# An attention output's last third visits four column strips of TensorE in turn, with new scheduler keys

## The chip, the cores and the metric

One core of a Trainium2 chip. The metric is the device time of one execution in microseconds (us), lower is better.

## The reference

A gated linear attention over 4 batches, 8 heads, 768 positions and head size 48, followed by two feed-forward layers (384 to 2048 to 384) over the 3072 tokens:

```python
for t in range(S):
    state = alpha[:, :, t, :, None] * state + np.einsum('bhd,bhe->bhde', k[:, :, t], v[:, :, t])
    y[:, :, t] = np.einsum('bhd,bhde->bhe', q[:, :, t], state)
...
h = x @ w_in
sp = np.where(h > 20.0, h, np.log1p(np.exp(np.minimum(h, 20.0))))
g = h * np.tanh(sp)
return (g @ w_out).astype(np.float32)
...
h = np.maximum(x @ w_in, 0.0)
return (h * h @ w_out).astype(np.float32)
```

## The kernel before, in words

**Attention.** The 768 positions are cut into 6 chunks `c` of 128; each chunk is done for each of the 4 batches `b`, 24 units (c, b) in all. For one unit, `a_load` and `a_loadv` fetch alpha, k, q (tile `akq`) and v; `a_prep`, `a_inv` and `a_k` run scans and products over them on VectorE (DVE; tiles `P`, `akq`); `a_kT` transposes k on TensorE; `a_scores` multiplies k by q and DVE masks the result into two tiles `at`, one for the even heads and one for the odd; `a_y` (line 538) makes the chunk's output on TensorE; `a_u` updates the state `st`; `a_x` splits the output into two halves `xh` and `xl`, which the first feed-forward layer reads.

**`a_y`.** The output of a unit is 384 rows, made as three thirds (`kk` = 0, 1, 2) of 128 rows by 128 positions in one PSUM bank. Each third is four strips of 32 rows (`i` = 0 to 3), and a strip is computed with 32 of TensorE's 128 columns. A strip of the first two thirds holds 32 rows of one head: for c > 0 one matmul with the state (`akq,st` in the profile) and one with the scores (`at,v`). A strip of the last third holds the remaining 16 rows of two heads: one matmul with the state and two with the scores. In chunk 0 there is no state, and only the matmuls with scores are made. All operands are 32-bit floats, and the trace has two records for each such matmul, here called two passes. So a unit of c > 0 has 28 matmuls and 56 passes, 32 of them in the first two thirds and 24 in the last; there are 20 such units.

**Feed-forward.** Weights come as 64-bit floats; `w_load`, `w_sign`, `w_abs`, `w_bits` and `w_split` turn a pair of weight blocks into `whi` and `wlo` (ScalarE, ACT, and DVE; tile `raw` before that). A step (c, f) is one block of 128 hidden units for one chunk: `h_mm` makes nine matmuls into one of three banks `ph`; `mish1`, `mish2` (ACT) and `mish3` (DVE: `u`, `y`, then `g`, which reads the bank last) apply the activation; `split_hi` and `split_lo` make `gh` and `gl`; `out1` adds nine matmuls to banks `pc`. The second layer follows after all 96 steps of the first, with `relu1` and `out2`.

**What sets the order.** Nothing is issued directly. `Recorder` notes each call as a unit of work with a cost from `price` (line 347), its queue (P TensorE, V VectorE, A ScalarE, G GpSimd, S the DMA queue) and a key. `Plan.order` (line 245) then plays the queues forward by these costs: of the units that could start within `SLACK` of the earliest, the one with the smallest key goes next. The keys are step numbers plus the offsets in the tables `FIRST_AT`, `EARLY_AT`, `LATER_AT`, `WEIGHT_AT` and `MLP_AT` (lines 36 to 41). All instructions are issued from line 321, so the profile's rows carry L321 and are told apart by their tiles.

The order of the passes of `a_y` is that of the loops `for kk`, `for i`, state first, then `for h in heads`.

Of the kernel before, what the change touches and what calls it, by code (L numbers as in the profile page):

```python
# [17 lines left out]
B, H, S, D = 4, 8, 768, 48  # L18
DM, DFF = 384, 2048
NT = B * S  # L20
CH = 128
# [5 lines left out]
CUT = ((slice(0, 32), slice(0, 32), slice(32, 64)), (slice(16, 48), slice(32, 64), slice(0, 32)))  # L27
# [2 lines left out]
WAIT = 0.2  # L30
SWITCH = 0.3
BYTE_SHIFTS = range(8)
SLACK = dict(P=4.68, V=0.01, A=0.18, G=0.10, S=3.45)


FIRST, EACH = -14.34, 4.47
FIRST_AT = dict(a_load=-8.92, a_loadv=-0.87, a_prep=-25.04, a_inv=-1.22, a_k=-40.25, a_kT=16.99, a_scores=-42.12, a_flag=-25.48, a_y=-7.03, a_u=-55.34, a_x=19.72)
EARLY_AT = dict(a_load=86.48, a_loadv=0.29, a_prep=-2.05, a_inv=1.20, a_k=-0.59, a_kT=-39.22, a_scores=-50.37, a_flag=29.17, a_y=-26.49, a_u=-16.63, a_x=-15.63)
LATER_AT = dict(a_load=-106.20, a_loadv=-63.70, a_prep=-101.21, a_inv=20.99, a_k=37.87, a_kT=-78.32, a_scores=-75.84, a_flag=23.67, a_y=2.78, a_u=-20.53, a_x=-24.76, b_load=-9.08, p_load=53.41)
WEIGHT_AT = dict(w_load=-16.99, w_sign=-7.37, w_abs=-52.56, w_bits=-0.61, w_split=-4.57)  # L40
MLP_AT = dict(mish1=42.39, mish2=0.64, mish3=1.90, hi=1.97, lo=-28.42, out=0.86)
EXP20 = 485165195.40979
NG = NF // 2

# [157 lines left out]
class Plan:  # L202
# [42 lines left out]
    def order(self):  # L245
        units = self.units
        users = {name: {i for i, _, _ in self.uses[name]} for name in self.tag_of}
        left = {name: len(x) for name, x in users.items()}
        nth, made, begun, freed = {}, {}, {}, {}
        for u in units:  # L250
            for name in u["new"]:
                tag = self.tag_of[name][0]
                nth[name] = made.get(tag, 0)
                made[tag] = nth[name] + 1
        held = [[] for _ in units]
        for name, x in users.items():
            for i in x:
                held[i].append(name)
        after = [[] for _ in units]
        for i, u in enumerate(units):  # L260
            u["after"] -= u["deps"]
            for j in u["deps"] | u["after"]:
                after[j].append(i)
        wait = [len(u["deps"] | u["after"]) for u in units]
        start, done, base = ([0.0] * len(units) for _ in range(3))
        free = dict.fromkeys("PVAGS", 0.0)
        shared, mode = 0.0, None
        ready = {q: {i for i, u in enumerate(units) if u["queue"] == q and not wait[i]} for q in free}

        def buffers(i):  # L270

            t, seen = 0.0, {}
            for name in units[i]["new"]:
                tag, bufs = self.tag_of[name]
                n = begun.get(tag, 0) + seen.get(tag, 0)
                seen[tag] = seen.get(tag, 0) + 1
                if nth[name] != n or len(freed.get(tag, [])) <= n - bufs:
                    return None
                if n >= bufs:
                    t = max(t, sorted(freed[tag])[n - bufs])  # L280
            return t

        for _ in units:
            picks = []
            for q, pool in ready.items():
                found = []
                for i in pool:
                    t = buffers(i)
                    if t is not None:
                        found.append((max(free[q], base[i], t, shared if units[i]["port"] else 0.0), units[i]["key"], i))  # L290
                if found:
                    first = min(found)[0]
                    pick = min((x for x in found if x[0] <= first + SLACK[q]), key=lambda x: x[1:])
                    picks.append((first, q, pick))
            _, q, (t, _, i) = min(picks, key=lambda x: x[0])
            u = units[i]
            ready[q].discard(i)
            start[i] = t
            free[q] = t + u["cost"] + (SWITCH if u["mode"] != mode and q == "P" else 0.0)
            mode = u["mode"] or mode  # L300
            done[i] = free[q] + u["late"]
            if u["port"]:
                shared = free[q] + (0.08 if q == "V" else 0.0)
            for name in u["new"]:
                tag = self.tag_of[name][0]
                begun[tag] = begun.get(tag, 0) + 1
            for name in held[i]:
                left[name] -= 1
                if not left[name]:
                    freed.setdefault(self.tag_of[name][0], []).append(max(done[j] for j in users[name]))  # L310
            for j in after[i]:
                base[j] = max(base[j], done[i] if i in units[j]["deps"] else start[i])
                wait[j] -= 1
                if not wait[j]:
                    ready[units[j]["queue"]].add(j)
        return sorted(range(len(units)), key=lambda i: start[i])
# [30 lines left out]
def price(queue, op, args, kw):  # L347


    out = args[0]  # L350
    n = out.free_size()
    ins = [a for a in (*args[1:], *kw.values()) if hasattr(a, "ap") and a is not kw.get("accum_out")]
    wide = [a for a in ins if a.space != PSUM and a.free_size() > 8]
    if queue == "P":
        if op == "transpose":
            return 0.109, 0.2, False
        m, n = args[1].free_size(), args[2].free_size()
        if args[2].dtype == F32R:
            return n / 2200, 0.2, False
        return (0.085 if m == 32 else 0.052 if n == D else 0.107), 0.28, False  # L360
    if queue == "S":
        size = math.prod(out.shape) * mybir.dt.size(out.dtype)
        return size / 390e3, 2.7, False
    if queue == "A":
        return (0.06 if len(wide) < len(ins) else 0.11) + n / 1200 + (0.1 if "accum_out" in kw else 0), 0.13, False
    if queue == "V":
        if op == "memset":
            return 0.03, 0.07, False
        if op == "reciprocal":
            return 0.07 + n * 0.006, 0.11, False  # L370
        if "scan" in op:
            return n * 2.21e-3, 0.11, True
        if op == "tensor_scalar" and out.space != PSUM and len(wide) == len(ins):
            return 0.07 + n / 1920, 0.11, True
        return 0.072 + n / 960, 0.11, len(wide) > 1
    if op == "tensor_scalar":
        return 0.12 + n / 1024, 0.05, True
    if op == "memset":
        return 0.1 + n / 1200, 0.05, False
    return 0.1 + n * 2.3e-3, 0.05, True  # L380
# [14 lines left out]
def fast_kernel(ctx, tc, flags, akq, v, w1i, w1o, w2i, w2o, out):  # L395
    nc = Plan(tc.nc)
# [21 lines left out]
    st = const.tile([128, B, NP, 2, D], F32, name="st")  # L418
# [49 lines left out]
    vt, At, Pt, kT, at, yt, kt, qt, v0 = {}, {}, {}, {}, {}, {}, {}, {}, []  # L468
# [69 lines left out]
    def a_y(c, b):  # L538
        ps = abank(c, 2)
        for kk in range(NK):  # L540
            for i in range(4):
                o = ps[32 * i:32 * i + 32, CH * kk:CH * kk + CH]
                heads = (4 * kk + i,) if kk < 2 else (2 * i, 2 * i + 1)
                if c > 0:
                    p = heads[0] // 2
                    s2 = st[:, b, p, heads[0] % 2, CUT[heads[0] % 2][0]] if kk < 2 else st[:, b, p].rearrange("p j e -> p (j e)")[:, 32:64]
                    nc.tensor.matmul(o, s2, qt[c, b][:, p, :], start=True, stop=False, skip_group_check=True)
                for h in heads:
                    p, j = h // 2, h % 2
                    w = vt[c, b][:, h, CUT[j][1] if kk < 2 else CUT[j][2]]  # L550
                    nc.tensor.matmul(o, w, at[c, b, j][:, p, :], start=(c == 0 and h == heads[0]), stop=(h == heads[-1]), skip_group_check=True)
        yt[c, b] = ps

    def a_u(c, b):
# [151 lines left out]
    with tc.manual_schedule():  # L706
# [13 lines left out]
        def at_step(t, fn, *args, key=None):  # L720
            name = fn.__name__
            if key is None:
                c, b = args[0], args[1] if len(args) > 1 else 0
                if c == 0 and name[0] == "a":
                    key = FIRST + EACH * b + FIRST_AT[name]
                else:
                    key = t + (EARLY_AT if 0 < c < 3 and name[0] == "a" else LATER_AT)[name]
            slots.setdefault(math.floor(t), []).append((fn, args, key))
# [64 lines left out]
        for s in range(tot + LAG):  # L793
            ph = s // NA
            if s < tot:
                c, f = step(s)
                run(h_mm, 2 * ph, c, f, key=s)
                run(relu1 if ph else mish1, c, f, key=s + MLP_AT["mish1"])
            p = s - 1
# [6 lines left out]
            o = s - LAG  # L806
# [61 lines left out]
```

## Time and profile before

| | |
|---|---|
| time, median of 3 runs | 965.78 us (963.88 to 966.77) |
| the profiled execution: time, span | 966.28 us, 964.6 us |
| mean granted TensorE clock | 0.982 of full speed |
| busy: TensorE, its weight loads, DVE, ACT | 97%, 82%, 66%, 58% of the span |
| chain that ended last | TensorE 83%, ACT 7%, DVE 7% |

The span runs from the first to the last instruction. TensorE's busy time is a union of overlapping matmuls, so a busy TensorE can still be slow. Where the engine waited, a row says so in brackets, with what ended the wait.

### The profile page before, as it was taken

The numbers are of one execution on the slowest core, as the hardware profiler recorded it, in microseconds if no ns is written. First come the engines' busy times: TensorE is split into PE (matmuls) and PEld (weight loads), VectorE is DVE, ScalarE is ACT, GpSimd is POOL, SyncE is SP. The second block draws the span as 40 slices with busy tenths as digits, with TensorE's granted clock in tenths as the row PEclk, the third lists the DMA queues.
The fourth block names the chain that finished last, engine by engine and source line by source line (L and its number), as shares of the span: only waits on it lengthen the run. The fifth ranks groups of instructions, "written<-read, shape, count | busy, mean of one in ns | idle before, by whom it ended". The sixth has DMA issues, their size and how long they took to land.

```text
span 964.6 us, 14441 instructions
## 1 busy us (share of the span) xinstructions
PE 934.1 (97%) x5818; PEld 788.5 (82%) x5818; DVE 637.3 (66%) x1014; ACT 559.6 (58%) x1103; POOL 2.7 (0%) x10
## 2 busy tenths in 40 slices
PE   6888999999999999999999999999999999999996
PEld 5666777778888888878888889988999899999995
DVE  7899999998788887777679997343333343433332
ACT  4487998778666767677599865332332332422322
POOL 1000000000000000000000000000000000000000
PEclk7699999999999999999999999999999999999998
DMA  8145324340221211121032251010000100100001
GB/s 326 68 154 191 126 66 137 121 149 1 82 82 47 77 45 45 44 78 45 1 138 92 70 194 64 1 66 1 33 33 1 66 1 1 66 1 1 34 1 36
DMA packets 22075, 67.13 MB, mean 70 GB/s; under 512 B 1776, under 2 KB 4848, under 8 KB 22000
## 3 DMA queue, kind: packets, MB, share of 16 engines
q1 hardware_dynamic: 22000, 66.13, 19.6%
q8 instruction: 47, 0.77, 0.3%
q14 instruction: 28, 0.23, 0.1%
HBM read 55.90 MB, written 10.22 MB: 69 GB/s over the span
## 4 chain that ended last, share of the span: by engine, by line
PE 83%; ACT 7%; DVE 7%; issue 1%; DMA 1%; SPq 0%; DVEq 0%; ACTq 0%
PE ph L321 37%; PE pc L321 34%; PE pa L321 12%; ACT u L321 2%; ACT y L321 2%; ACT raw L321 1%; DVE akq L321 1%; ACT whi L321 1%; DVE raw L321 1%; DMA raw<-w1o 1%; DVE P L321 1%; DVE st L321 1%; ACT gh L321 1%; DVE gl L321 1%; ACT akq L321 1%
## 5 line engine op out<-in xcount | busy, mean ns | idle before, releaser
L321 PE MATMUL ph<-xh,wlo 128*128 128x512 f32 x576 | 230.1, 399 | 5.3 <-DVE g L321 2.7
L321 PE MATMUL ph<-xh,whi 128*128 128x512 f32 x576 | 228.0, 396 | 0.0
L321 PE MATMUL ph<-xl,whi 128*128 128x512 f32 x576 | 227.9, 396 | 0.0
L321 DVE TENSOR_TENSOR gl<-g,gh 128x512 fp32r<-128x512 f32 x192 | 131.9, 687 | 127.2 <-ACT gh L321 126.7
L321 ACT ACTIVATE u<-ph 128x512 f32<-128x512 f32 x192 | 113.8, 593 | 170.0 <-PE ph L321 163.4
L321 ACT ACTIVATE gh<-g 128x512 fp32r<-128x512 f32 x192 | 120.2, 627 | 135.1 <-PE pa L321 112.8
L321 DVE TENSOR_TENSOR g<-u,ph 128x512 f32<-128x512 f32 x96 | 66.0, 687 | 118.6 <-ACT u L321 118.6
L321 PEld LDWEIGHTS ph<-xh,wlo 128*128 128x128 f32 x576 | 108.7, 189 | 28.7 <-DVE g L321 4.4
L321 PEld LDWEIGHTS ph<-xh,whi 128*128 128x128 f32 x576 | 108.5, 188 | 25.4
L321 PEld LDWEIGHTS ph<-xl,whi 128*128 128x128 f32 x576 | 108.5, 188 | 20.6
L321 PE MATMUL pc<-gh,wlo 128*128 128x512 f32 x288 | 117.0, 406 | 0.9 <-ACT x L321 0.9
L321 PE MATMUL pc<-gh,whi 128*128 128x512 f32 x288 | 113.6, 394 | 0.0
L321 PE MATMUL pc<-gl,whi 128*128 128x512 f32 x288 | 113.1, 393 | 0.0
L321 DVE SCALAR_TENSOR_TENSOR u<-u,y 128x512 f32<-128x512 f32 x96 | 65.8, 686 | 50.4 <-ACT y L321 50.1
L321 PE MATMUL pc<-wlo,gh 128*128 128x384 f32 x288 | 97.0, 337 | 0.0
L321 PE MATMUL pc<-whi,gh 128*128 128x384 f32 x288 | 97.0, 337 | 0.0
L321 PE MATMUL pc<-whi,gl 128*128 128x384 f32 x288 | 96.9, 337 | 0.0
L321 DVE SCALAR_TENSOR_TENSOR g<-y,ph 128x512 f32<-128x512 f32 x96 | 65.4, 681 | 1.6
L321 PEld LDWEIGHTS pc<-gh,wlo 128*128 128x128 f32 x288 | 54.1, 188 | 14.8 <-ACT x L321 1.3
L321 DVE SCALAR_TENSOR_TENSOR y<-u,y 128x512 f32<-128x512 f32 x96 | 65.7, 685 | 0.7
L321 PEld LDWEIGHTS pc<-gh,whi 128*128 128x128 f32 x288 | 54.0, 187 | 13.2
L321 PEld LDWEIGHTS pc<-gl,whi 128*128 128x128 f32 x288 | 54.1, 188 | 12.1 <-DVE gl L321 0.6
(90 smaller groups left out, 1261.6 us busy)
## 6 DMA issues: line engine op xcount, KB each, us to landing
akq<-akq SPq DMA_DIRECT2D x20, 770.5 KB, 4.5
raw<-w1i SPq DMA_DIRECT2D x8, 768.0 KB, 4.6
v<-v SPq DMA_DIRECT2D x24, 256.0 KB, 4.4
raw<-w1o SPq DMA_DIRECT2D x8, 768.0 KB, 4.3
raw<-w2i SPq DMA_DIRECT2D x8, 768.0 KB, 4.4
raw<-w2o SPq DMA_DIRECT2D x8, 768.0 KB, 4.3
x2d<-x SPq DMA_DIRECT2D x7, 768.0 KB, 3.5
x<-x2d SPq DMA_DIRECT2D x7, 768.0 KB, 4.3
```

What stands on the lines that cost most here:

```text
L321: method(*args, **kw)
```

## The change

`a_y` is written with the strips in the inner loop: for each third, the four state matmuls, then the first scores matmul of each strip, then (last third only) the second scores matmul of each strip. The number, shape and operands of the matmuls are the same. The price of a 32-column matmul in `price` falls from 0.085 to 0.06; a TensorE unit that depends on another TensorE unit may now follow it at once (before, 0.2 or 0.28 us later); and `SLACK`, `FIRST`, `EACH` and the five tables of keys have new numbers.

```diff
-SLACK = dict(P=4.68, V=0.01, A=0.18, G=0.10, S=3.45)
+SLACK = dict(P=7.05, V=0.00, A=0.15, G=0.10, S=5.68)
...
-FIRST, EACH = -14.34, 4.47
+FIRST, EACH = -14.93, 4.00
...
-                base[j] = max(base[j], done[i] if i in units[j]["deps"] else start[i])
+                same = units[j]["queue"] == "P" == u["queue"]
+                base[j] = max(base[j], free["P"] if same else done[i] if i in units[j]["deps"] else start[i])
...
-        return (0.085 if m == 32 else 0.052 if n == D else 0.107), 0.28, False
+        return (0.06 if m == 32 else 0.052 if n == D else 0.107), 0.28, False
...
-            for i in range(4):
-                o = ps[32 * i:32 * i + 32, CH * kk:CH * kk + CH]
-                heads = (4 * kk + i,) if kk < 2 else (2 * i, 2 * i + 1)
-                if c > 0:
-                    p = heads[0] // 2
-                    s2 = st[:, b, p, heads[0] % 2, CUT[heads[0] % 2][0]] if kk < 2 else st[:, b, p].rearrange("p j e -> p (j e)")[:, 32:64]
-                    nc.tensor.matmul(o, s2, qt[c, b][:, p, :], start=True, stop=False, skip_group_check=True)
-                for h in heads:
+            groups = [(4 * kk + i,) if kk < 2 else (2 * i, 2 * i + 1) for i in range(4)]
+            o = [ps[32 * i:32 * i + 32, CH * kk:CH * kk + CH] for i in range(4)]
+            for i, heads in enumerate(groups if c > 0 else ()):
+                p, j = heads[0] // 2, heads[0] % 2
+                s2 = st[:, b, p, j, CUT[j][0]] if kk < 2 else st[:, b, p].rearrange("p j e -> p (j e)")[:, 32:64]
+                nc.tensor.matmul(o[i], s2, qt[c, b][:, p, :], start=True, stop=False, skip_group_check=True)
+            for n in range(len(groups[0])):
+                for i, heads in enumerate(groups):
+                    h = heads[n]
                     p, j = h // 2, h % 2
                     w = vt[c, b][:, h, CUT[j][1] if kk < 2 else CUT[j][2]]
-                    nc.tensor.matmul(o, w, at[c, b, j][:, p, :], start=(c == 0 and h == heads[0]), stop=(h == heads[-1]), skip_group_check=True)
+                    nc.tensor.matmul(o[i], w, at[c, b, j][:, p, :], start=(c == 0 and n == 0), stop=(h == heads[-1]), skip_group_check=True)
```

What this does to the order of the instructions is shown at three places. In these rows `xN` is N equal instructions in a row, and the numbers tell the tiles apart.

**TensorE, the first unit of chunk 1: the last third of `a_y`.** `pa` is the output's bank, `st` the state, `at_197` the scores of the even heads and `at_198` those of the odd. Before (the last strip of the second third, then the last third):

```order
L321 MATMUL pa_209<-akq_159,st_109 32x128
L321 MATMUL pa_209<-at_198,v_160 32x128
L321 MATMUL pa_209<-akq_159,st_109 32x128
L321 MATMUL pa_209<-at_197,v_160 32x128
L321 MATMUL pa_209<-at_198,v_160 32x128
L321 MATMUL pa_209<-akq_159,st_109 32x128
L321 MATMUL pa_209<-at_197,v_160 32x128
L321 MATMUL pa_209<-at_198,v_160 32x128
```

Now (from the second third's scores on):

```order
L322 MATMUL pa_209<-akq_159,st_109 32x128 x4
L322 MATMUL pa_209<-at_197,v_160 32x128
L322 MATMUL pa_209<-at_198,v_160 32x128
L322 MATMUL pa_209<-at_197,v_160 32x128
L322 MATMUL pa_209<-at_198,v_160 32x128
L322 MATMUL pa_209<-akq_159,st_109 32x128 x4
L322 MATMUL pa_209<-at_197,v_160 32x128 x4
L322 MATMUL pa_209<-at_198,v_160 32x128 x4
```

Before, a strip of the last third has its three matmuls (six passes) in a row, and the next strip follows; now each strip has one matmul (two passes) at a time. In the first two thirds it was two matmuls (four passes) in a row, and is now one.

**DVE, around 130 us: the `g` of step 14 (`g_343`), after which the bank `ph_335` is free for step 17.** Before:

```order
L321 TENSOR_TENSOR gl_340<-g_337,gh_339 128x512
L321 TENSOR_TENSOR wlo_347<-raw_315,whi_346 128x768
L321 SCALAR_TENSOR_TENSOR u_336<-u_336,y_338 128x512
L321 SCALAR_TENSOR_TENSOR P_390<-akq_373,reset_108 128x516
L321 SCALAR_TENSOR_TENSOR y_338<-u_336,y_338 128x512
L321 RECIPROCAL reset_108<-P_390 128x4
L321 SCALAR_TENSOR_TENSOR u_342<-u_342,y_344 128x512
L321 SCALAR_TENSOR_TENSOR g_343<-y_338,ph_335 128x512
```

Now:

```order
L322 SCALAR_TENSOR_TENSOR u_336<-u_336,y_338 128x512
L322 SCALAR_TENSOR_TENSOR raw_333<-raw_333 128x768
L322 TENSOR_TENSOR gl_340<-g_337,gh_339 128x512
L322 SCALAR_TENSOR_TENSOR y_338<-u_336,y_338 128x512
L322 SCALAR_TENSOR_TENSOR u_342<-u_342,y_344 128x512
L322 SCALAR_TENSOR_TENSOR g_343<-y_338,ph_335 128x512
```

The scan that makes `P` (named SCALAR_TENSOR_TENSOR here, TENSOR_TENSOR_SCAN in the trace) and its reciprocal no longer stand ahead of this `g`. Counted to this `g`, DVE's queue holds 197 instructions before and 193 now: those missing are one scan `P`, one reciprocal, one scan back over `akq` and one small memset. Counted to the `g` that frees a bank for step 8, it holds the same 138 in both.

**The DMA queue (SP), its first loads.** Before:

```order
L321 DMA raw<-w1i 128x2x768
L321 DMA v<-v 128x512
L321 DMA raw<-w1i 128x2x768
L321 DMA akq_136<-akq 128x517
L321 DMA akq_136<-akq 128x512 x2
```

Now:

```order
L322 DMA raw<-w1i 128x2x768
L322 DMA akq_136<-akq 128x517
L322 DMA akq_136<-akq 128x512 x2
L322 DMA v<-v 128x512
L322 DMA raw<-w1i 128x2x768
```

The first `v`, which the first `a_y` of all reads, now stands behind the three loads of the third batch's alpha, k and q.

## Rows read from the trace of the kernel before

**Rows 1.** The page, part 1: busy time, share of span, instructions.

```profile
PE 934.1 (97%) x5818; PEld 788.5 (82%) x5818; DVE 637.3 (66%) x1014; ACT 559.6 (58%) x1103; POOL 2.7 (0%) x10
```

**Rows 2.** Stretches: length, busy of PE, PEld, DVE, ACT, POOL, granted clock, DMA.

```profile
45.00:100.00 55.00, 48.90 (x471) 38.04 (x471) 51.98 (x87) 43.96 (x89) 0.00 (x0) 0.99 0.47 163
100.00:150.00 50.00, 47.93 (x275) 37.68 (x275) 48.63 (x73) 47.94 (x96) 0.00 (x0) 1.00 0.33 110
150.00:205.00 55.00, 53.20 (x439) 41.78 (x438) 52.99 (x91) 43.56 (x90) 0.00 (x0) 1.00 0.34 119
205.00:480.00 275.00, 275.00 (x1983) 221.67 (x1982) 215.96 (x362) 191.19 (x391) 0.00 (x0) 1.00 0.16 54
```

**Rows 3.** Waits of PE from 45 to 205 us: total, times, longest.

```profile
PE ph L321 <- DVE g L321: 2.7, 3, 1.2
PE ph L321 <- DVE wlo L321: 2.5, 4, 1.1
PE pa L321 <- DVE at L321: 2.2, 2, 1.4
```

**Rows 4.** Timeline of PE, one a_y at 304.71: start, length, operation.

```profile
304.71 0.45 PE L321 MATMUL pa<-akq,st 128*32 128x128 f32 x8
304.95 0.42 PE L321 MATMUL pa<-at,v 128*32 128x128 f32 x8
305.17 0.44 PE L321 MATMUL pa<-akq,st 128*32 128x128 f32 x8
305.39 0.44 PE L321 MATMUL pa<-at,v 128*32 128x128 f32 x8
305.60 0.38 PE L321 MATMUL pa<-akq,st 128*32 128x128 f32 x2
...
305.83 0.30 PE L321 MATMUL pa<-akq,st 128*32 128x128 f32 x1
...
306.08 0.30 PE L321 MATMUL pa<-akq,st 128*32 128x128 f32 x1
...
306.33 0.30 PE L321 MATMUL pa<-akq,st 128*32 128x128 f32 x1
...
306.54 0.63 PE L321 MATMUL pa<-at,v 128*32 128x128 f32 x6
307.10 0.38 PE L321 MATMUL pa<-v,kT 128*64 128x48 f32 x6
```

**Rows 5.** The unit's first weight loads in the timeline, and all 480 by line.

```profile
304.70 0.18 PEld L321 LDWEIGHTS pa<-akq,st 128*32 128x32 f32 x8 [0.37 <-issue]
...
L321 PEld LDWEIGHTS pa<-akq,st 128*32 128x32 f32 x480 | 22.2, 108 | 9.7 <-issue 5.8 <-DVE at L321 3.9
```

**Rows 6.** Two stretches, PE's matmuls on the state alone: busy (passes).

```profile
45.00:100.00 55.00, 8.10 (x96) 0.99 0.47 163
205.00:480.00 275.00, 24.18 (x288) 1.00 0.16 54
```

**Rows 7.** Stretch of the third a_y of chunk 0, columns as in rows 2.

```profile
26.00:28.50 2.50, 2.42 (x32) 1.56 (x32) 2.50 (x6) 0.48 (x2) 0.00 (x0) 0.51 0.10 36
```

**Rows 8.** Timeline of DVE and PE near 133 us.

```profile
130.59 1.22 DVE L321 TENSOR_TENSOR_SCAN P<-akq,reset 128x516 f32<-128x516 f32 x1
...
132.98 0.68 DVE L321 SCALAR_TENSOR_TENSOR g<-y,ph 128x512 f32<-128x512 f32 x1
...
133.71 0.50 PE L321 MATMUL ph<-xh,wlo 128*128 128x512 f32 x1 [1.21 <-DVE g L321]
```

**Rows 9.** Timeline of DVE and PE near 93 us (step 8).

```profile
92.30 0.68 DVE L321 SCALAR_TENSOR_TENSOR g<-y,ph 128x512 f32<-128x512 f32 x1
...
93.03 0.50 PE L321 MATMUL ph<-xh,wlo 128*128 128x512 f32 x1 [1.20 <-DVE g L321]
```

**Rows 10.** An early stretch (columns as in rows 2) and the first a_y.

```profile
9.00:15.00 6.00, 4.74 (x66) 3.53 (x62) 5.36 (x9) 4.27 (x10) 0.00 (x0) 0.72 1.03 401
...
11.28 1.86 PE L321 MATMUL pc<-at,v 128*32 128x128 f32 x32
```

More of the change, by code (lines that the diff above doesn't have):

```diff
@@ L32 @@
 BYTE_SHIFTS = range(8)
-SLACK = dict(P=4.68, V=0.01, A=0.18, G=0.10, S=3.45)
-FIRST, EACH = -14.34, 4.47
[L37 to L41, printed above, removed]
+SLACK = dict(P=7.05, V=0.00, A=0.15, G=0.10, S=5.68)
+FIRST, EACH = -14.93, 4.00
+FIRST_AT = dict(a_load=-8.68, a_loadv=0.02, a_prep=-37.05, a_inv=-13.25, a_k=-39.85, a_kT=33.23, a_scores=-49.10, a_flag=-6.53, a_y=-34.31, a_u=-42.28, a_x=37.52)
+EARLY_AT = dict(a_load=99.85, a_loadv=5.05, a_prep=-0.05, a_inv=1.71, a_k=1.12, a_kT=-63.76, a_scores=-47.66, a_flag=19.98, a_y=-47.34, a_u=-12.07, a_x=-7.79)
+LATER_AT = dict(a_load=-126.00, a_loadv=-30.46, a_prep=-114.98, a_inv=24.77, a_k=34.64, a_kT=-64.62, a_scores=-73.56, a_flag=52.32, a_y=1.01, a_u=-32.29, a_x=-28.66, b_load=-1.77, p_load=31.72)
+WEIGHT_AT = dict(w_load=-16.68, w_sign=-4.58, w_abs=-49.46, w_bits=-1.04, w_split=-13.78)
+MLP_AT = dict(mish1=40.66, mish2=0.43, mish3=1.83, hi=2.10, lo=-25.92, out=0.13)
 EXP20 = 485165195.40979
```

## The prediction

> **What bounds the kernel now.** I read the page first: TensorE is busy 97% of the span, DVE 66%, ACT 58% [rows 1]. A share over the whole span hides stages, so the second view is the table of stretches [rows 2]. It shows two regimes. From 205 to 480 us TensorE is busy for all of 275.00 us, DVE for 215.96 and ACT for 191.19: here TensorE alone sets the pace, and whatever it no longer has to do comes off the end. From 45 to 205 us DVE is busy for 51.98 of 55, 48.63 of 50 and 52.99 of 55 us, and TensorE misses 6.1, 2.1 and 1.8 us. The view of waits says on what: mostly on DVE's `g`, `wlo` and `at`, 2.7, 2.5 and 2.2 us [rows 3]. There DVE bounds as much as TensorE does, and a faster TensorE may only wait longer.
>
> The third view is the timeline of one `a_y` of chunk 1 or later [rows 4]; the reader should compare it with the program's order. The program gives a strip of the first two thirds four passes in a row, but the trace starts eight passes on the state (two on each strip), then eight on the scores: four strips run side by side, and these 32 passes take from 304.71 to 305.60, 0.89 us, or eight turns of 0.111 us in which every strip does one pass. The last third gives a strip six passes in a row, and the picture breaks: the first passes of its four strips start at 305.60, 305.83, 306.08 and 306.33, about 0.24 us apart, that is two turns. It reads as if four passes of a strip may be outstanding and the stream stands still behind the fifth: a strip with six must finish two before the next strip's first can enter. So the last third, with 24 passes, lasts from 305.60 to 307.10, 1.50 us, against 0.89 for 32 passes.
>
> **The change, part by part. The strips.** No matmul, load or DMA is added or removed. In turn, each strip has two passes, then the next; no strip ever has more than four ahead of a waiting one, so the last third should run as the others do: six turns. Its last turn starts at 305.60 + 5 x 0.111 = 306.16. Within a turn the fourth strip starts some 0.05 us after the first (the first eight passes last 0.45 us, of which one turn is 0.11 and one pass 0.27 to 0.30), so the last pass starts at 306.21. Before, the last pass started at 306.54 + 0.63 - 0.27 = 306.90, and the next work at 307.10, 0.20 later. The same 0.20 gives 306.41: **0.69 us saved per unit**. The bounds are 0 (the order does not matter) and 0.83 (1.50 less six turns, with no tail). I take 0.69, since two thirds of this very unit run so.
>
> The Trainium skill, "TensorE: Matmul & The Clock Gate" (Part 3, "What overlaps and what doesn't"), says that weight loads overlap running matmuls only where the row group differs; here all strips use all 128 rows. By that rule the strips could not run side by side, the order would not matter, and this term would be 0 instead of 0.69. The trace disagrees: eight loads of 0.108 us each, 0.86 in a row, pass in 0.18 us [rows 5].
>
> Chunk 0 has two matmuls, four passes, per strip in its last third and gains nothing: 32 passes take 2.42 us there at half the clock (granted 0.51) [rows 7]; eight turns at that clock are 8 x 0.22 = 1.8, and one after the other they would be 7.1.
>
> The 20 units lie as follows [rows 5, 6]: a unit has 24 passes on the state, so of the 480, 288 after 205 us are 12 units, 96 from 45 to 100 us are 4, and the other 96, between 100 and 205 us, are 4.
>
> - Twelve units after 205 us: 12 x 0.69 = 8.3 us. Nothing covers this, TensorE never waits there. DVE and ACT have 59 and 84 us to spare in 275, so TensorE stays the bound.
> - Four units from 100 to 205 us: 2.8 us. Bounds 0 (DVE, 52.99 of 55 us busy, holds it) and 2.8 plus some waits. I take 2.8, because TensorE misses only 2.1 and 1.8 us there.
> - Four units from 45 to 100 us: 0. Step 8 starts at 93.03, when DVE's `g` at 92.30 is done, after a wait of 1.20 [rows 9]; the same 138 DVE instructions stand up to that `g` now, on a DVE busy for 51.98 of 55 us. If TensorE is earlier, it waits for the same `g`. Bounds: all four count, 2.8; or the opening loses 2.0 (next item).
>
> **The new keys.** They reorder the queues; none adds work. Two places can be priced. At 133.71 TensorE waits 1.21 us for `g`, and 1.22 us of the DVE work ahead of that `g` is the scan `P` [rows 8], which now stands behind it: 1.2 us saved, what comes next being ACT, 47.94 of 50 us busy in that stretch. In the opening, the first `v` is loaded behind 770.5 KB more; at 401 GB/s [rows 10] that is 2.0 us, and the first `a_y`, at 11.28, would wait up to that long; behind it in TensorE's queue stand `a_u` and the next scores, for which DVE's state update and mask wait. DVE has weight work moved up that fills part of the gap, and later loads come earlier by what this one lost. I take 0, with 2.0 lost as the bound. The other differences are of the same kind, one DVE instruction before or behind another, and I give them 0: gains up to the waits that rows 3 sum, 7.4 us, less the 1.2 already counted, would be the extreme; I use a third of it, 2.1, in the range.
>
> The sum: 8.3 + 2.8 + 0 + 1.2 = 12.3 us. The profiled execution took 966.28 (span 964.6 and 1.7 around it), which gives 954.0. The median is 965.78, 0.5 lower, so **953.5**.
>
> **The rivals.** *DVE keeps everything before 205 us.* For it: DVE is busy 96% there. Against it: TensorE misses little after 100 us. Only 8.3 us come through: 957.5. Chance 0.17.
>
> *The keys also recover the opening.* All 20 units count, 13.8, with 1.2 at 133 us and 2.1 of the other waits, 17.1 in all: 948.7. For it: every wait in rows 3 hangs on the order of DVE's queue, which is rewritten. Against it: the 138 instructions up to step 8. Chance 0.18.
>
> *The order of strips does not matter.* It would if what looks like a limit per strip is a limit of the stream as a whole, or the weight loads; then only the 1.2 us at 133 us remain: 964.6. The start of eight passes on four strips within 0.2 us speaks against it. Chance 0.04. This is also what the Trainium skill's rule above would give.
>
> *Slower: a change of strip has a price.* Before, a unit changes strip 11 times, now 27. If each change let the array run dry for as long as the step from one unit's end to the next work, 0.20 us less a turn, 0.09, the 16 more would cost 1.4 us against 0.69 saved: 20 x 0.75 = 15 us slower, 981. It decides from 0.69 / 16 = 0.043 us per change on. Against it: in [rows 4] passes of four strips lie in one turn of 0.111 already. Chance 0.02. Another 0.02 goes to keys that open new waits of more than 12 us.
>
> **How the numbers follow.** The forecast has 0.57, and spans 950.5 to 956.5 by the bounds of the two early groups of units and of the opening. The rivals have 0.17, 0.18, 0.04, 0.02 and 0.02. The range, 948.5 to 958.0, takes in the forecast, the first rival and nearly all of the second. A measurement of this kernel tells 0.3%, 2.9 us, from no change: faster by more is 0.57 + 0.17 + 0.18 and a part of the rest, 0.93; same 0.04; slower 0.03.
>
> **What would show it.** In the changed kernel's timeline one `a_y` of chunk 1 or later should start eight passes on the state in the last third too, and be followed by the next work 1.71 us after its start (306.41 less 304.71) instead of 2.39. The stretch after 205 us should still show TensorE busy throughout. The wait for `g` near 133 us should be gone, and one near step 8 as long as before or longer. I am wrong if the last third still starts its strips 0.24 us apart, if TensorE shows waits after 205 us, or if the total of its waits from 45 to 205 us differs from before by more than 3 us.

## The result and the profile after

The changed kernel takes 954.69 us (median of 4 runs, 952.95 to 957.69) beside 965.25 for the kernel before (4 runs): a ratio of 0.9894, with a 95% interval of [0.9864, 0.9923]. Two repeats on other chips gave 954.04 beside 966.04, 0.9875 [0.986, 0.9891], and 953.19 beside 964.41, 0.9881 [0.9864, 0.9898]. It is 1.1 to 1.25% faster; 953.5 was forecast. The profiled execution took 952.95, span 951.2; it is the fastest of its four runs.

The page, part 1, answers to [rows 1]: TensorE is busy 13.8 us less (934.1 before), and the same 97% of its span.

```profile
PE 920.3 (97%) x5818; PEld 776.7 (82%) x5818; DVE 636.4 (67%) x1014; ACT 558.5 (59%) x1103; POOL 2.7 (0%) x10
```

The stretches of the changed kernel, columns as in [rows 2]:

```profile
45.00:100.00 55.00, 47.56 (x463) 37.53 (x462) 51.62 (x87) 42.26 (x83) 0.00 (x0) 0.91 0.48 164
100.00:150.00 50.00, 49.80 (x212) 38.76 (x211) 48.01 (x72) 49.26 (x97) 0.00 (x0) 1.00 0.28 95
150.00:205.00 55.00, 53.63 (x524) 42.38 (x523) 54.28 (x96) 40.36 (x87) 0.00 (x0) 1.00 0.47 161
205.00:466.00 261.00, 260.95 (x1959) 208.65 (x1958) 213.42 (x357) 187.61 (x389) 0.00 (x0) 1.00 0.15 51
```

After 205 us TensorE still sets the pace alone (260.95 of 261). From 45 to 205 us it now misses 7.4, 0.2 and 1.4 us; before, 6.1, 2.1 and 1.8. The total hardly differs, but it has moved ahead of 100 us. There the granted clock is 0.91, where it was 0.99.

One `a_y` in TensorE's timeline, to be held against [rows 4]:

```profile
293.80 0.43 PE L322 MATMUL pa<-akq,st 128*32 128x128 f32 x8
294.04 0.40 PE L322 MATMUL pa<-at,v 128*32 128x128 f32 x8
294.26 0.40 PE L322 MATMUL pa<-akq,st 128*32 128x128 f32 x8
294.48 0.40 PE L322 MATMUL pa<-at,v 128*32 128x128 f32 x8
294.70 0.40 PE L322 MATMUL pa<-akq,st 128*32 128x128 f32 x8
294.92 0.62 PE L322 MATMUL pa<-at,v 128*32 128x128 f32 x16
295.46 0.67 PE L322 MATMUL pa<-v,kT 128*64 128x48 f32 x16
```

The last third now starts like the others, eight passes on the state at 294.70. The next work follows the unit's start by 295.46 - 293.80 = 1.66 us (before, 307.10 - 304.71 = 2.39): 0.73 us saved.

TensorE's waits from 45 to 205 us, columns as in [rows 3]:

```profile
PE ph L322 <- DVE g L322: 2.6, 3, 1.4
PE pa L322 <- issue: 1.5, 1, 1.5
PE ph L322 <- DVE wlo L322: 1.1, 1, 1.1
PE pa L322 <- ACT kT L322: 1.0, 3, 0.4
...
PE pa L322 <- DVE at L322: 0.4, 1, 0.4
```

DVE's `g` costs as much as before, `wlo` and `at` together 3.2 us less; smaller waits have taken part of their place. In the opening a wait for the first `v` is new:

```profile
PE pc L322 <- DMA v<-v: 2.7, 1, 2.7
```

Two lines of TensorE's timeline stand where [rows 8] and [rows 9] do. The wait of 1.21 us at step 17 (133.71) is gone; one for `g` stands at step 7:

```profile
89.31 0.50 PE L322 MATMUL ph<-xh,wlo 128*128 128x512 f32 x1 [1.44 <-DVE g L322]
...
132.00 0.39 PE L322 MATMUL ph<-xh,wlo 128*128 128x512 f32 x1
```

### The profile page after: what moved, and what is told of

Read it like the earlier page. It is cut to its first block, busy times and chain, and to the rows that moved or that the text cites. A ratio compares the mean times of both kernels' runs of the same rounds, so it can differ in the third digit from the quotient of the medians.

```text
span 951.2 us, 14425 instructions
## 1 busy us (share of the span) xinstructions
PE 920.3 (97%) x5818; PEld 776.7 (82%) x5818; DVE 636.4 (67%) x1014; ACT 558.5 (59%) x1103; POOL 2.7 (0%) x10
## 4 chain that ended last, share of the span: by engine, by line
PE 87%; DVE 6%; ACT 4%; issue 1%; DMA 1%; SPq 0%; DVEq 0%
PE ph L322 39%; PE pc L322 36%; PE pa L322 12%; ACT u L322 1%; DVE akq L322 1%; DVE raw L322 1%; DMA v<-v 1%; DVE st L322 1%; ACT raw L322 1%; DVE at L322 1%; ACT y L322 1%; DVE wlo L322 1%; DVE g L322 1%; DVE P L322 0%; SPq L322 0%
## 5 line engine op out<-in xcount | busy, mean ns | idle before, releaser
L322 PE MATMUL pc<-gl,whi 128*128 128x512 f32 x288 | 113.1, 393 | 0.0
L322 PEld LDWEIGHTS pc<-gh,whi 128*128 128x128 f32 x288 | 54.0, 188 | 13.2
## 6 DMA issues: line engine op xcount, KB each, us to landing
akq<-akq SPq DMA_DIRECT2D x20, 770.5 KB, 4.6
```

The costliest lines, as they stand in the source:

```text
L322: method(*args, **kw)
```

## The experiments

The time of a step is below always the start of its first matmul `ph<-xh,wlo`, counted from the start of the span: before, step 8 is the one at 93.03, step 17 the one at 133.71.

**The two parts of the change apart.** `strips_alone` is the kernel before with the new `a_y`; the order of all else is as before. `keys_only` is the changed kernel with the old `a_y`; every other queue is in the changed kernel's order.

```
strips_alone: before, with
+            groups = [(4 * kk + i,) if kk < 2 else (2 * i, 2 * i + 1) for i in range(4)]
...
+            for n in range(len(groups[0])):
+                for i, heads in enumerate(groups):
keys_only: the change without these lines
```

> Only the loops of a_y are the new ones; prices, keys and so the order of every other instruction are the old ones. Theory (strips save 0.73 us in each of 20 units, DVE holds what is saved before about 134 us, and part of what is saved from there to 205 us): a_y of chunk 1 or later followed by the next work after 1.67 us instead of 2.40; step 8 still starts near 93.0 us and step 17 near 133.7; twelve units after 205 us give 8.8 us, the four between 100 and 205 us 0 to 2.9. Time 953.6 to 956.5 us. Rival (the new keys carry half of the gain): 959 to 961 us.

Measured: 957.56 us, 0.9914 [0.9896, 0.9931], units of 1.67 us. The time is 1.1 us above the range that the theory gave, and below its rival's.

> Prices, rule and keys are the new ones, and a_y has its old loops; every queue but TensorE's inside a_y has the new order. Theory: the keys are worth 0 to 2.5 us by themselves, so 963 to 966 us, and the difference to the changed kernel is 8.8 to 11.7 us. Rival (the new keys carry half of the gain): 959 to 961 us.

Measured: 965.91 us, 0.9995 [0.9983, 1.0007], units of 2.40 us, in the range of the theory.

> The changed kernel once more, for a closer comparison beside the two halves: 952 to 957 us. If the half clock that the trace showed near 71 us belongs to this order of instructions, it shows again; if it is chance, it is gone.

Measured: 954.04 us, 0.9875 [0.986, 0.9891]. So the strips alone take off 8.5 us, the keys alone 0.1, and both 12.0: some 3.4 us belong to neither part by itself (each of the three intervals reaches 1.2 to 1.7 us to either side). How long the stretches between steps are in one profile of each, and in all three of the changed kernel, shows in part where:

```
us from step to step  before  strips_alone  keys_only  change  change again  change third
start to 8              93.0          92.1       94.2    93.6          96.6          96.1
8 to 30                119.6         119.4      114.4   113.1         113.1         113.1
30 to 82               272.0         264.3      273.4   264.7         264.7         264.7
82 to 192              460.4         460.4      460.4   460.4         460.4         460.4
192 to the end          19.6          19.4       19.4    19.4          19.4          19.5
```

With the old keys the strips save 0.2 us of the 2.9 that four units should give from step 8 to 30, and 7.7 of 8.8 from 30 to 82. Most of the missing time is in new waits. Those of TensorE in `strips_alone` from 100 to 205 us, which sum to 5.6 us (3.8 before):

```profile
PE pa L321 <- issue: 2.1, 2, 1.2
PE ph L321 <- DVE g L321: 1.1, 1, 1.1
PE pc L321 <- ACT x L321: 0.8, 1, 0.8
PE pa L321 <- DVE at L321: 0.8, 1, 0.8
PE pa L321 <- PE ph L321: 0.5, 1, 0.5
...
```

and after 205 us, where the kernel before has none:

```profile
PE pa L321 <- issue: 0.5, 1, 0.5
PE pa L321 <- DVE xl L321: 0.3, 1, 0.3
```

With the new keys the same view of `keys_only` from 100 to 205 us has three waits, 0.6 us in all (the changed kernel has 1.6):

```profile
PE pa L322 <- ACT kT L322: 0.2, 1, 0.2
PE ph L322 <- DVE g L322: 0.2, 1, 0.2
PE pa L322 <- PE pc L322: 0.2, 1, 0.2
```

Between step 8 and 30 the keys save 5.2 us alone, but 1.4 of them are work that was moved. Between the starts of those two steps the trace has 784 matmul records before and 768 in `keys_only`; the 16 that are missing there, one unit's scores (`pa<-akq`), stand behind step 30. Before:

```profile
209.30 1.16 PE L321 MATMUL pa<-akq 48*128 48x128 f32 x16
...
212.59 0.39 PE L321 MATMUL ph<-xh,wlo 128*128 128x512 f32 x1
```

and in `keys_only`:

```profile
208.62 0.48 PE L322 MATMUL ph<-xh,wlo 128*128 128x512 f32 x1
...
210.89 1.16 PE L322 MATMUL pa<-akq 48*128 48x128 f32 x16
```

So the stretch from step 30 to 82 is 1.4 us longer under the new keys (273.4 against 272.0), with no wait of TensorE in either. From step 8 to 82 together the keys alone save 3.8 us, and the change 13.8. Under the new keys the strips bring 1.3 of 2.9 us from step 8 to 30 and 8.7 of 8.8 after it.

Ahead of step 8 the keys lose: 1.2 us in `keys_only`'s profile, and more by the medians. From step 8 to the end the three profiles of the changed kernel agree within 0.1 us (857.6), so what differs between its executions lies ahead of step 8. An estimate takes the same stretch as fixed in the kernel before (871.5) and in `keys_only` (867.6) too, of which there is one profile each. Then `keys_only`, which wins 4.0 us behind step 8 and 0.1 in its median, has lost 3.9 ahead of it. The changed kernel, which wins 13.9 behind it and 10.6, 12.0 and 11.2 in its three medians, has lost 3.3, 1.9 and 2.7.

**The late first v.** The new keys put the first `v` behind 770.5 KB more. `v_ahead` is the changed kernel with this one load issued ahead of them:

```
+        first = next(i for i in loads if self.units[i]["calls"][0][1][0].name.startswith("v"))
+        seq.remove(first)
+        seq.insert(seq.index(loads[7]), first)
```

> The changed kernel with one DMA moved: the first v is issued where it was before the change, ahead of the three loads of the third batch. Theory (the late v costs the opening, 2.7 us of wait before the first a_y): that wait falls to about 0.5 us or less, the first a_y starts near 11.3 instead of 12.66 us, and step 1 starts up to 1.4 us earlier; the end gains between 0 (DVE holds it again) and 1.4 us. Rival (what the opening waits for is DVE, and the load is hidden): step 1 at 40.6 us as before.

Measured: 954.09 us, 0.9876 [0.986, 0.9891], beside 954.04 without it. The first `a_y` starts at 11.00 instead of 13.11, but step 1 only 0.9 us earlier (40.2, 41.1; the other two profiles of the changed kernel have 40.6 and 41.3), step 8 0.5 us (96.1, 96.6), and the end not measurably. The opening's late load costs nothing at the end.

**How many passes a strip may have outstanding.** `four_in_row` gives a strip its state and first score passes at once in each third; `eight_in_row` puts the first two thirds together, eight passes in a row on a strip, with the last third in turn.

```
four_in_row
-            for i, heads in enumerate(groups if c > 0 else ()):
...
+            for half in range(2 if kk == 2 else 1):
+                for i in range(4):
eight_in_row
-        for kk in range(NK):
...
+        for i in range(4):
+            for kk in range(2):
```

> The changed kernel, with each third of a unit written so that a strip gets its state passes and its first score passes, four in a row, before the next strip's turn. Theory (a strip can have four passes outstanding, and the stream stands only behind a fifth): the unit stays at 1.65 to 1.75 us, the time within 1.5 us of the changed kernel's 954.1. Rival (only two passes of a strip run freely, any longer row stands): the second turn of each third is lost, 0.2 us or more a third, so a unit of 2.2 us or more and 6 us or more at the end (960 or above).

Measured: 956.18 us, 0.9909 [0.9889, 0.993]; the unit takes 1.72 us. The unit is as the theory has it; the time is 2.1 us above the changed kernel's in another batch of runs, 0.6 more than expected. Twenty units of 0.05 us more explain 1.1 of it. From step 8 to the end its profile is 0.7 us longer than the changed kernel's; the rest lies ahead of step 8, where the changed kernel's own profiles differ by 3.0.

> The changed kernel, with the first two thirds put together so that each strip gets eight passes in a row (state and score passes of both thirds), the last third in turn as now. Theory (four outstanding, a pass of one strip 0.108 us after the one before it): strips start 4 x 0.108 = 0.43 us apart, the unit grows by 3 x 0.43 = 1.3 us to about 3.0 us, at least 12 x 1.3 = 16 us at the end (970 to 981). Rival (the order of the strips does not matter, what the last third gained was a matter of its own operands): the unit stays near 1.67 us and the time near 954.

Measured: 974.84 us, 1.0093 [1.0074, 1.0113]: slower than the kernel before. One unit in TensorE's timeline:

```profile
236.91 0.41 PE L322 MATMUL pa<-akq,st 128*32 128x128 f32 x2
237.16 0.38 PE L322 MATMUL pa<-at,v 128*32 128x128 f32 x2
237.37 0.41 PE L322 MATMUL pa<-akq,st 128*32 128x128 f32 x4
237.59 0.41 PE L322 MATMUL pa<-at,v 128*32 128x128 f32 x4
237.84 0.41 PE L322 MATMUL pa<-akq,st 128*32 128x128 f32 x4
238.06 0.41 PE L322 MATMUL pa<-at,v 128*32 128x128 f32 x4
238.31 0.41 PE L322 MATMUL pa<-akq,st 128*32 128x128 f32 x4
238.53 0.41 PE L322 MATMUL pa<-at,v 128*32 128x128 f32 x4
238.77 0.43 PE L322 MATMUL pa<-akq,st 128*32 128x128 f32 x8
...
239.96 0.44 PE L322 MATMUL pa<-v,kT 128*64 128x48 f32 x8
```

The first strip runs four passes alone (two at 236.91, two at 237.16). At 237.37 its fifth starts, and with it the first pass of the second strip: the group of that start has four passes, two of either strip. The third strip enters at 237.84, the fourth at 238.31, 0.47 us apart each, and only where all four have entered, at 238.77, do groups of eight appear. The unit takes 3.05 us (3.0 was expected). Three layouts say the same: with four passes in a row on a strip all strips run side by side, with six (before) the next enters two turns late, with eight four turns late. The limit that fits all three is four outstanding passes a strip, the running one counted, with the stream standing behind the fifth. Every matmul here has two passes, so whether four passes or two matmuls are counted no run shows, nor which queue holds them. By the rule of the Trainium skill that the prediction named ("TensorE: Matmul & The Clock Gate", Part 3, "What overlaps and what doesn't") the order would not matter, the loads of all strips being on the same 128 rows; three orders of the same matmuls took 1.67, 2.40 and 3.05 us, so the measurement decides against it here.

**TensorE's clock at 70 us.** The prediction did not foresee this. The changed kernel in 5 us pieces (TensorE's busy time, granted clock, DMA share, GB/s):

```profile
65.00:70.00 5.00, 3.10 (x23) 0.89 0.09 37
70.00:75.00 5.00, 4.63 (x76) 0.50 0.01 3
```

and the kernel before:

```profile
65.00:70.00 5.00, 3.28 (x51) 1.00 0.34 137
70.00:75.00 5.00, 4.43 (x61) 1.00 0.28 71
```

TensorE is idle for 1.9 us between 65 and 70 us, 1.5 of them ahead of transposes of k that start at 67.18, 0.10 us after DVE's product `akq` is done; it then runs 70 to 75 us at 0.50, the lower of its two levels (1.2 of 2.4 GHz); the `a_y` there takes 3.31 us instead of 1.67. It is so in all three profiles of the changed kernel (the `a_y` takes 3.00 in the second), and in part in `strips_alone` (0.74) and `keys_only` (0.66). In the two later profiles of the changed kernel 80 to 85 us run at 0.50 too. In the repeat a landing of `akq` 1.8 us after DVE was ready for it comes on top. Does the half clock cost time at the end? Five runs, with four kernels, put extra products of the identity matrix by itself into the bank of the transposes of batches 2 and 3 of chunk 1, where TensorE idles. `fill(ps, n)` issues n of them into the bank's first 128 columns, at no cost for the planner, so that the order of all else stays:

```
     def a_kT(c, b):
         ps = abank(c, 0)
+        fill(ps, {(1, 2): 14, (1, 3): 8}.get((c, b), 0))
fill_long: 28 and 12 of them, and in a_y
+        fill(ps, 4 if (c, b) in ((1, 2), (1, 3)) else 0)
fill_few: 8 and 2
fill_few_akq: as fill_few, and
+        seq.remove(loads[26])
+        seq.insert(seq.index(loads[27]) + 1, loads[26])
```

> The changed kernel with 14 and 8 extra products of the identity matrix by itself (0.109 us each, into the same bank) ahead of the transposes of batches 2 and 3 of the second chunk, where TensorE stood idle at 66 to 70 us and at 77 us, and the granted clock was 0.50 behind it; the order of everything else is unchanged. Theory (the half clock follows the idle time and costs time at the end): the clock of 70 to 75 us rises from 0.50 to 0.8 or more, the units there take 1.7 us instead of 3, the eighth step starts 2 to 3 us earlier and the end comes 1.5 to 3 us earlier (951 to 952.5). Rival (VectorE's chain sets this stretch whatever the clock): clock up, end within 0.7 us of 954.1. Second rival: these products fill too little and the clock falls all the same, no change.

Measured: 952.89 us, 0.9874 [0.9858, 0.989]; clock 1.00 throughout 60 to 90 us. The time lies between what the theory and its first rival gave.

> As fill_short, with 28 and 12 of them, and 4 ahead of each of the two units' own products. Theory: as fill_short, with the clock at 0.9 or more over 65 to 90 us; where the products outlast the wait (28 x 0.109 = 3.1 us against waits of 1.5 and 3.3 us in two profiles) they cost up to 1.6 us themselves, so 951 to 954. Rival (VectorE's chain sets it): within 0.7 us of 954.1, or up to 1.6 us later.

Measured: 958.32 us, 0.9923 [0.9908, 0.9938], outside what either theory gave. The size in the expectation was wrong: a product is two passes, and the 28 took 6.41 us, not 3.1. TensorE then came 4.3 us late for DVE, as DVE's timeline shows:

```profile
75.81 1.29 DVE L324 TENSOR_TENSOR at<-pa,mask 128x512 f32<-128x512 f32 x2 [4.32 <-PE pa L324]
```

> The changed kernel once more, on the chip of the next three, so that they can be told from it: 953 to 955, clock 0.50 in 70 to 75 us.

Measured: 953.19 us, 0.9881 [0.9864, 0.9898]; clock 0.50 at 70 to 75 us.

> fill_short again, beside the changed kernel. Theory (the half clock costs about 1 us net at the end): 0.7 to 1.5 us faster than after_third. Rival (the 952.9 of the first run came from its chip): within 0.5 us of after_third.

Measured: 953.53 us, 0.9882 [0.9863, 0.99], 0.3 us slower than `after_third`: the rival's case.

> Eight and two products of the identity matrix instead of 14 and 8. A product is two passes, 28 of them took 3.29 us in fill_short, and the keys of batch 2 were ready 1.1 us before the last of them ended; eight take 0.23 x 8 = 1.9 us. Theory: the clock stays at 1.00 over 65 to 85 us and the eighth step starts about 1 us earlier than in fill_short, 0.5 to 1.5 us at the end. Rival (the short fill leaves the clock to fall): 0.50 or so again in 70 to 75 us and the time of after_third. Second rival (the wait for VectorE's g at the eighth step takes it up): as fill_short.

Measured: 952.87 us, 0.9882 [0.9864, 0.9899], 0.7 us below `fill_short_two` with the same ratio. The clock is full:

```profile
65.00:70.00 5.00, 3.83 (x27) 1.00 0.18 73
70.00:75.00 5.00, 3.87 (x86) 1.00 0.02 3
```

> As fill_few, and the load of the third batch of the second chunk issued ahead of the weight load that stood 0.43 us before it on the queue. In two of the profiles of the changed kernel VectorE waited 0 and 1.8 us for it. Theory (the sixth to eighth steps differ between profiles by this landing): it lands before it is asked for, up to 1.8 us earlier at the eighth step and 0 to 1.5 us at the end against fill_few. Rival: the weight load is then late by as much, no difference, or up to 1 us slower.

Measured: 952.86 us, 0.9876 [0.9859, 0.9894]; DVE no longer waits for that `akq`; the clock is 1.00 from 60 to 75 us, then 0.95 and 0.70. The time does not differ from `fill_few`'s, as the rival had it.

With the idle time filled, 70 to 75 us run at 1.00 in each of the five profiles: it is what TensorE does ahead of it that brings the half clock on. In the profiles it shortens the way from step 5 to 8: 32.2, 34.7 and 34.0 us in the three of the changed kernel, 31.4, 31.4, 30.4 and 30.6 in the short fillings. In the medians of one chip nothing of it can be told: 953.19 without, 953.53, 952.87 and 952.86 with, and the intervals coincide. By the estimate above, the changed kernel has lost 2.7 us ahead of step 8 on that chip, and these three fillings 2.6, 2.0 and 2.1, so by it the half clock is not most of the loss. Whether a few tenths of a microsecond are left stays open, and no version is shown to beat the changed kernel.

## Why the prediction was right, and where its sum was not

**The strips: right, 0.04 us too small.** 0.69 us a unit was taken from the thirds that already ran in turn; 0.73 was measured. The reading behind it, four outstanding passes a strip, held in both runs made to break it; the unit was at 1.72 us with four in a row and at 3.05 with eight.

**Twelve units after 205 us: right.** 8.3 was forecast; under the new keys the strips bring 273.4 - 264.7 = 8.7 from step 30 to 82, and TensorE waits nowhere there.

**Four units from 100 to 205 us, and the keys: the sum fell short, its division was wrong.** The forecast was 2.8 for the strips, "because TensorE misses only 2.1 and 1.8 us there", and 1.2 for the keys, 4.0 together; from step 8 to 30 the change saves 6.5, of which 1.4 is the scores moved behind step 30, so 5.1. By themselves the strips bring 0.2 there, and 957.56 in all, which is the first rival's 957.5. That DVE is what kept the gain, as this rival has it, is shown in part only: of the 5.6 us of waits from 100 to 205 us the view puts 2.2 down to DVE (2.3 before) and 2.1 to `issue` (0.6 before). That TensorE misses little says how much it waits now, not how much an earlier TensorE would wait; the 2.8 came through only in part even under the new keys (114.4 - 113.1 = 1.3). The keys bring 5.2 - 1.4 = 3.8, of which the waits from 100 to 205 us give 3.2 (3.8 before, 0.6 in `keys_only`); only the wait at 133 us was in the sum. The other differences of the keys had been given 0, with no more than 2.1 in the range.

**Four units ahead of step 8 and the opening: the step "0" failed, by up to 3.6 us.** Step 8 starts not at 93.0; it is at 93.6, 96.6 and 96.1 in three profiles, in two of them past the bound of 2.0 lost. A wait for DVE's `g` stands near it, as forecast, but the reason given, that the same 138 DVE instructions stand up to the `g` that step 8 needs, does not fix the time of that step, for two reasons. Before, step 8 starts 0.05 us after this `g` ends; now it starts 0.8 us after it in all three profiles. The wait has moved to step 7 (the 1.44 us at 89.31), whose `g` is the 133rd of DVE's instructions where it was the 126th, and step 8 follows 4.3 us behind step 7 without a wait. And the `g` of step 8 itself ends at 92.8, 95.8 and 95.3 instead of 93.0. Up to its end DVE is busy for the same time, 82.4 us before and 82.5, 82.6 and 82.8 now, but it stands idle for 10.6 us before and for 10.3, 13.2 and 12.5 now. What it waits for from 45 us on has changed. Before, on ACT and nowhere on TensorE:

```profile
DVE raw L321 <- ACT raw L321: 2.0, 1, 2.0
```

and in the third profile of the changed kernel on TensorE:

```profile
DVE st L322 <- PE pa L322: 3.6, 2, 2.0
DVE at L322 <- PE pa L322: 0.6, 1, 0.6
```

In the three profiles these waits for TensorE sum to 2.7, 3.3 and 4.2 us, in `keys_only` to 3.1 and in `strips_alone` to nothing: they come with the new keys. The number of DVE's instructions was taken for their time, and TensorE's queue, which feeds them, was left out. The mechanism named for the bound, the late `v`, is not it: `v_ahead` takes that away and wins 0.5 us. The half clock from 70 us on and, in one profile, a landing of `akq` 1.8 us late lengthen these waits in single profiles: DVE's `st` waits 2.3, 2.4 and 3.6 us for TensorE in the three, and 0 to 0.4 in the four short fillings. In the medians of the filled kernels nothing of it could be told. What else in the new order costs the time stays open.

**The sum.** After step 30 the keys neither cost nor bring anything but the moved scores. From step 8 on the change saves 13.9 us where 12.3 were forecast (1.1 more between steps 8 and 30, 0.4 more from the strips after it, 0.1 in the last stretch), and ahead of step 8 it loses 1.9 to 3.3 by the estimate above where 0 was forecast. So 12.3 came out near the 10.6, 12.0 and 11.2 measured because the two errors have opposite signs. The time was right for the largest term; the rest was luck as much as reading.

**What was to be seen.** The next work comes 1.66 us after a unit's start (1.71 forecast); TensorE is busy throughout after 205 us; the wait at 133 us is gone; one for `g` near step 8 is there, 1.44 us long (1.20 before); TensorE's missing time from 45 to 205 us is 9.0 us against 10.0, within the 3 us allowed.

## What to carry to other kernels

Where several column strips of TensorE work side by side, write their matmuls in turn, with no more than four passes in a row for a strip: the same work took 1.67, 2.40 or 3.05 us here by its order alone. A gain on TensorE came through in full here only where TensorE waits for nothing; where DVE is as busy, 0.2 us of 2.9 came through under the old order and 1.3 under the new, so time the two parts apart and together. Before a stretch between two marks is called faster or slower, count the work in it: 1.4 us here had only moved across a mark. Waits seen in one profile, a late load or a clock that falls, are worth nothing until a run without them is faster.

## What the runs showed that was not expected

Passes on one strip start 0.109 us apart (the last four of the unit in `eight_in_row`), those of different strips, in one turn of the units shown of the kernel before and of the changed kernel, 0.005 to 0.014 us apart. TensorE's clock fell to 0.50 in the changed kernel after 65 to 70 us, in which TensorE was busy for 3.10 us (first profile) and 1.66 us (repeat); before the change it was busy for 3.28 us of the same stretch, and the clock stayed at 1.00. In `four_in_row` it fell to 0.50 after 3.34 us of it. At the half clock a unit took 3.31 us in place of 1.67. A product of two 128 x 128 matrices in 32 bits took 3.29 / 14 = 0.23 us, as two passes.
